# A seven-column sum moved into the unused columns of its neighbour tile, in a one-core attention and gated-convolution kernel

## The chip, the core and the metric

The kernel runs on one core of a Trainium2 chip. The metric is the device time of one execution in microseconds (us); the median of several runs counts, and lower is better. Engines are named as in the profile: PE multiplies matrices, PEld is its weight loading, DVE is the vector engine, ACT the scalar engine (activation functions and copies), POOL the general one, and SP issues all the DMAs.

## What is computed

For 8 batches of 12 heads, with 448 rows and a head width of 64, soft-capped attention is followed by a gated convolution and two projections of width 768. Cut to the core, the reference is:

```python
scores = scale * np.matmul(q, k.transpose(0, 1, 3, 2))
scores = cap * np.tanh(scores / cap)
attn = np.exp(scores - np.max(scores, axis=-1, keepdims=True))
attn = attn / (np.sum(attn, axis=-1, keepdims=True) + 1e-09)
x = np.matmul(attn, v)                 # heads side by side: (8, 448, 768)
gate = sigmoid(sum of conv_w[k] * x shifted by k rows, five taps)
out = (gate * (x @ w_val)) @ w_out
```

## The kernel before, in words

**Pairs and blocks.** Two heads make a pair of 128 partitions, so there are 48 pairs p, six to a batch. For each pair q and k are loaded by SP and turned by DVE (L455). The scores go through PE in four parts of 112 rows (L476), ACT takes tanh (L484) and exp (L488) of each part into a tile `pt`, and PE multiplies by v (L514). For pairs 0 to 12 the scores are plain float32 products of `qt` and `kt`; from pair 13 on, q and k are split into a high and a low half (`qh`, `ql`, `kh`, `kl`, the high halves by ACT at L461, the low ones by DVE at L390) and three faster products are added up. The sums of the exponentials over a row come from a product with ones (L530). For most pairs DVE first adds the four parts to one or two (`pa`, L498 and L495), so that PE has less to do there.

**The normalisation of a pair** is a short chain across DVE and POOL, and the change lies in it. `turn_sums` turns the 224 columns of sums into the tile `zt` (L536), which is 448 columns wide. `norm_recip` adds the guard 1e-9 to seven of these columns, one in 32 (L543, result `zc`), and takes the reciprocal of the seven twice over into `rc` (L544). `shift` lets POOL copy parts of `rc` between partitions (L551, L552), `spread` turns `rc` out over all 448 columns of `zt` (L557), and `norm_mul` multiplies the attention's output by it into `u` (L565). There are two tiles `u`, one for even pairs and one for odd ones.

**After the pair.** ACT rounds `u` to `xh` (L570), DVE takes the rest `xl` (L390), and DVE convolves five taps into a tile `gate` (L582 or L584, then four times L586). For each batch PE multiplies `xh` and `xl` by the first weights (L607 to L609, 448 columns each; the weights are the part that stays in the array, `xh` or `xl` the part that is streamed), DVE multiplies the result by the gate (L613), the gated values are split once more (`g_h` by ACT at L616, `g_l` by DVE at L390), and PE multiplies them by the second weights (L636 to L638, where 384 columns of `wo` are streamed). ACT copies the result to `osb` (L644) and SP stores it.

**What sets the order.** Three tables of numbers give every step of every pair, batch and weight block a due time; the steps are sorted by it and written to the engines' queues in that order. Each engine works through its queue strictly in order, and semaphores hold an instruction until its inputs are there. The change touches none of these tables.

**What sets the addresses.** A pool lays out its tiles in each partition in the order of the line that first asks for each name, with the number of buffers asked for, and rounds each tile up to a multiple of 32 bytes. In the pool `wk` the order is `qt`, `kt`, `pt` (6 buffers), `zt`, `rc`, `zc`, `gate` (7), `xh` (8), `xl` (8), `pa` (2) and `osb` (2). Behind this pool lie, first, the scratch tiles for the weights (`w_raw`, `w_late`, `w_t`), and later, in the same place, the halves `qh`, `kh`, `ql`, `kl`. Ahead of the pool lie the inputs' tiles, the weights `wv` and `wo`, the gated tiles `g_h` and `g_l`, and the tiles `u`.

The built program's addresses, taken modulo 64 bytes, fall into two classes. `zc` starts at byte 160672 of each partition and takes 32 bytes; the first `gate` follows at 160704, which is 2511 times 64. All tiles behind it are multiples of 64 bytes long where it matters (448 float32 are 28 times 64 bytes, 896 are 56 times), so `gate`, `xh`, `xl`, `pa`, `osb`, `qh`, `kh`, `ql`, `kl` and `w_raw` all start at a multiple of 64. Of the tiles ahead, `qt`, `kt`, `pt`, `zt`, `rc`, `zc`, `vn`, `ones`, `wv`, `wo`, `g_h`, `g_l` and the even pairs' `u` start 32 bytes past one, and the odd pairs' `u` starts at one.

The lines that the change and the prediction's steps touch:

Of the kernel before, what the change touches and what calls it, by code (L numbers as in the profile page):

```python
# [7 lines left out]
F32 = mybir.dt.float32  # L8
# [13 lines left out]
P = 128  # L22
# [326 lines left out]
def fast_path(tc, io, u2, q, k, v, w_val, conv_w, w_out, out, capt):  # L349
# [22 lines left out]
    HQ = S * BLK // D  # L372
    HC = HQ // BLK

    with ExitStack() as ctx:
        cpool = ctx.enter_context(tc.tile_pool(name="cpool", bufs=1))
        wk = ctx.enter_context(tc.tile_pool(name="wk", bufs=2))
# [160 lines left out]
        def norm_recip(p):  # L538
            st = state[p]
            rc = wk.tile([P, D // BLK, HC], F32, name="rc", bufs=1)  # L540
            zc = wk.tile([P, HC], F32, name="zc", bufs=1)
            col = st["zt"].rearrange("p (c e) -> p c e", e=BLK)[:, :HC, 0]
            nc.vector.tensor_scalar(zc, col, guard, None, ALU.add)  # L543
            nc.vector.reciprocal(rc, zc.unsqueeze(1).to_broadcast([P, D // BLK, HC]))  # L544
            st["rc"] = rc
# [109 lines left out]
        def at(when, f, *a):  # L655
# [7 lines left out]
            q_hi=lambda p: half_hi("q", p), k_hi=lambda p: half_hi("k", p),  # L663
            q_lo=lambda p: half_lo("q", p), k_lo=lambda p: half_lo("k", p),
            scores=scores, tanh=tanh, exp=exp, add=add, av=attnv, sums=sums, turn_sums=turn_sums, recip=norm_recip, shift=shift,
            spread=spread, mul=norm_mul, x_hi=x_hi, x_lo=x_lo, conv=conv,
        )
# [205 lines left out]
```

## Time and profile before

| what | value |
|---|---|
| median of 3 runs | 710.95 us (710.48 to 710.96) |
| the profiled execution's own time | 710.17 us |
| its span, first to last instruction | 708.3 us |
| PE busy | 689.1 us, 97% of the span |
| ACT busy | 576.5 us, 81% |
| DVE busy | 557.7 us, 79% |
| POOL busy | 76.6 us, 11% |

A row of the profile's groups names the line, the engine, the operation and its tiles as output<-inputs, then output and input shapes, the number of instructions, the union of their busy time in us and the mean time of one in ns, and behind the next bar the engine's idle time ahead of them with what ended it. For PE, durations overlap, since the next product enters the array before the last has left it: there the distance from start to start, in the timeline, is what an instruction costs. The chain of waits follows the execution back from its last instruction, at each step to what released it.

### The profile page before, as it was taken

Reading aid. Unit: us, or ns where it says so; the run is one execution under the profiler, and the core shown is the slowest. Engines: PE = TensorE matmul, PEld = TensorE weight load, DVE = VectorE, ACT = ScalarE, POOL = GpSimd, SP = SyncE. Lnnn points to the kernel's source line nnn. Section 1 sums busy time; section 2 is a strip of 40 time slices with the busy share of each in tenths; the row PEclk is TensorE's granted clock in tenths of the full one; section 3 lists DMA queues with packets and bytes.
Section 4 is the critical chain, followed back from the end, with each engine's and each line's share of the span. In section 5 each row is a group of like instructions: output and inputs, shape, how many; then the busy total and the mean of one; then the engine's idle time right before and its main releaser. Section 6 shows DMA issues by size and latency. Waiting matters only on the chain.

```text
span 708.3 us, 13291 instructions
## 1 busy us (share of the span) xinstructions
PE 689.1 (97%) x5024; PEld 481.2 (68%) x5024; DVE 557.7 (79%) x972; ACT 576.5 (81%) x738; POOL 76.6 (11%) x208
## 2 busy tenths in 40 slices
PE   5889999999999999999999999999999999999997
PEld 1233567567768776767768777587767867776997
DVE  1698999998798878987787887988889696887520
ACT  5999999898887798798895799879897689986211
POOL 0021101120001002100000010130001010120000
PEclk9999999999999999999999999999999999999999
DMA  7999998852415414134213352333323333101011
GB/s 138 175 217 217 225 219 187 226 112 55 76 27 122 81 32 82 35 86 88 64 30 72 87 107 47 53 72 67 64 51 53 95 65 64 38 25 45 12 35 58
DMA packets 241829, 63.88 MB, mean 90 GB/s; under 512 B 228448, under 2 KB 235616, under 8 KB 241760
## 3 DMA queue, kind: packets, MB, share of 16 engines
q1 hardware_dynamic: 241760, 62.98, 41.5%
q8 instruction: 41, 0.67, 0.4%
q14 instruction: 28, 0.23, 0.1%
HBM read 51.94 MB, written 11.01 MB: 89 GB/s over the span
## 4 chain that ended last, share of the span: by engine, by line
PE 85%; ACT 9%; SPq 2%; DVE 1%; DMA 1%; issue 1%; ACTq 0%
PE psa L514 17%; PE pss L476 16%; PE psf L607 9%; PE psf L636 8%; PE psf L608 8%; PE psf L609 8%; PE psf L638 8%; PE psf L637 8%; ACT pt L484 3%; ACT pt L488 3%; PE psz L530 2%; SPq L333 1%; ACT L488 1%; DMA qn<-in_q_dram 1%; SPq L307 1%
## 5 line engine op out<-in xcount | busy, mean ns | idle before, releaser
L484 ACT ACTIVATE pt<-pss,rc 112x896 f32<-112x896 f32 x192 | 187.9, 1003 | 39.8 <-PE pss L476 37.2
L488 ACT ACTIVATE pt<-pt,capt 112x896 f32<-112x896 f32 x192 | 194.5, 1042 | 1.2
L514 PE MATMUL psa<-pt,vn 112*32 112x448 f32 x1440 | 150.3, 542 | 0.0
L586 DVE SCALAR_TENSOR_TENSOR gate<-u,cw,gate 128x448 f32<-128x448 f32 x192 | 125.6, 663 | 1.0 <-ACT gate L582 0.2
L636 PE MATMUL psf<-wo,g_h 128*128 128x384 f32 x336 | 115.2, 343 | 0.0
L638 PE MATMUL psf<-wo,g_l 128*128 128x384 f32 x336 | 112.7, 335 | 0.2 <-DVE g_l L390 0.2
L637 PE MATMUL psf<-wo,g_h 128*128 128x384 f32 x336 | 112.5, 335 | 0.0
L607 PE MATMUL psf<-xh,wv 128*128 128x448 f32 x288 | 108.2, 376 | 0.1
L498 DVE TENSOR_TENSOR pa<-pt 112x896 f32<-112x896 f32 x84 | 90.9, 1086 | 19.9 <-ACT pt L488 19.6
L608 PE MATMUL psf<-xh,wv 128*128 128x448 f32 x288 | 105.8, 368 | 0.0
L609 PE MATMUL psf<-xl,wv 128*128 128x448 f32 x288 | 105.8, 367 | 0.0
L551 POOL COPY rc<-rc 32x7 f32<-32x7 f32 x96 | 33.2, 346 | 555.2 <-DVE rc L544 553.2
L514 PEld LDWEIGHTS psa<-pt,vn 112*32 112x32 f32 x1440 | 42.3, 109 | 71.6 <-issue 58.4
L636 PEld LDWEIGHTS psf<-wo,g_h 128*128 128x128 f32 x336 | 63.0, 188 | 10.1 <-issue 7.5
L644 ACT COPY osb<-psf 128x384 f32<-128x384 f32 x56 | 26.5, 477 | 45.6 <-PE psf L638 44.2
L638 PEld LDWEIGHTS psf<-wo,g_l 128*128 128x128 f32 x336 | 63.1, 188 | 0.5 <-DVE g_l L390 0.5
L607 PEld LDWEIGHTS psf<-xh,wv 128*128 128x128 f32 x288 | 54.0, 188 | 13.6 <-issue 5.8
L637 PEld LDWEIGHTS psf<-wo,g_h 128*128 128x128 f32 x336 | 63.1, 188 | 0.1
L476 PE MATMUL pss<-qt,kt 64*112 64x448 f32 x208 | 49.5, 587 | 12.6 <-DVE guard L399 7.9
L476 PE MATMUL pss<-qh,kh 64*112 64x448 f32 x280 | 58.0, 410 | 0.0
L609 PEld LDWEIGHTS psf<-xl,wv 128*128 128x128 f32 x288 | 54.0, 188 | 5.1
L608 PEld LDWEIGHTS psf<-xh,wv 128*128 128x128 f32 x288 | 54.1, 188 | 4.5
(76 smaller groups left out, 908.1 us busy)
## 6 DMA issues: line engine op xcount, KB each, us to landing
vn<-in_v_dram SPq DMA_DIRECT2D x96, 112.0 KB, 2.8
out_dram<-osb SPq DMA_DIRECT2D x56, 192.0 KB, 2.2
kn<-in_k_dram SPq DMA_DIRECT2D x188, 56.0 KB, 2.4
qn<-in_q_dram SPq DMA_DIRECT2D x188, 56.0 KB, 2.4
w_raw<-in_moe_w_val_dram SPq DMA_DIRECT2D x12, 384.0 KB, 3.9
w_late<-in_moe_w_val_dram SPq DMA_DIRECT2D x12, 384.0 KB, 4.2
w_raw<-in_moe_w_out_dram SPq DMA_DIRECT2D x12, 384.0 KB, 3.6
w_late<-in_moe_w_out_dram SPq DMA_DIRECT2D x12, 384.0 KB, 4.3
```

Source lines behind the costliest of these rows:

```text
L476: nc.tensor.matmul(ps[:CH, j, :S], st[x][r, c], st[y][r], start=(n == 0), stop=(n == len(parts) - 1))
L484: nc.scalar.activation(st["p", i], st.pop(("s", i)), AF.Tanh, scale=rc8[:CH])
L488: nc.scalar.activation(t, t, AF.Exp, scale=capt[:CH])
L498: nc.vector.tensor_tensor(st["a", i], st["p", 2 * i], st["p", 2 * i + 1], op=ALU.add)
L514: nc.tensor.matmul(st["o"][r, :S], vloads[p][:, j, i, d:d + BLK], t[:, j], start=(i == 0), stop=(i == NKT - 1))
L586: nc.vector.scalar_tensor_tensor(g, u[:, i:i + S], cw[:, hp, i:i + 1], g, ALU.mult, ALU.add)
L607: nc.tensor.matmul(o, w_h, xh, start=(c == 0), stop=False)
L608: nc.tensor.matmul(o, w_l, xh, start=False, stop=False)
L609: nc.tensor.matmul(o, w_h, xl, start=False, stop=(c == NCC - 1))
L636: nc.tensor.matmul(o, g_h[:, d, s], w_h, start=(d == 0), stop=False)
L637: nc.tensor.matmul(o, g_h[:, d, s], w_l, start=False, stop=False)
L638: nc.tensor.matmul(o, g_l[:, d, s], w_h, start=False, stop=(d == NCC - 1))
```

## The change

The guarded sums no longer have a tile of their own. They are written to columns 224 to 230 of `zt`, which hold nothing at that point: the turned sums fill columns 0 to 223, and `spread` writes all 448 columns later.

```diff
         def norm_recip(p):
             st = state[p]
             rc = wk.tile([P, D // BLK, HC], F32, name="rc", bufs=1)
-            zc = wk.tile([P, HC], F32, name="zc", bufs=1)
+            zc = st["zt"][:, HQ:HQ + HC]
             col = st["zt"].rearrange("p (c e) -> p c e", e=BLK)[:, :HC, 0]
             nc.vector.tensor_scalar(zc, col, guard, None, ALU.add)
             nc.vector.reciprocal(rc, zc.unsqueeze(1).to_broadcast([P, D // BLK, HC]))
```

`HQ` is 224 and `HC` is 7. The queue of DVE at the first pair, before (-) and after (+), with the engines that each instruction waits for in brackets:

```order
 L536 STREAM_TRANSPOSE zt<-psz 128x224 [waits PE_49]
-L543 TENSOR_SCALAR zc<-zt,guard 128x7 [waits DVE_49]
-L544 RECIPROCAL rc<-zc 128x14 [waits DVE_49]
+L543 TENSOR_SCALAR zt<-zt,guard 128x7 [waits DVE_49]
+L544 RECIPROCAL rc<-zt 128x14 [waits DVE_49]
 L557 STREAM_TRANSPOSE zt<-rc 128x448 [waits DVE_49,Pool_49]
```

Nothing moves here, and nowhere else: apart from the output of L543 and the input of L544, all 48 times, the two programs have the same instructions in the same order, with the same semaphores waited for up to the same counts.

What does move is addresses. With `zc` gone, every tile behind it starts 32 bytes earlier: the first `gate` at 160672 instead of 160704. So `gate`, `xh`, `xl`, `pa`, `osb`, `qh`, `kh`, `ql`, `kl` and the weights' scratch now start 32 bytes past a multiple of 64, as most tiles ahead of them do. The tiles ahead, and all tiles in the accumulation memory, stay where they were. The new place of the seven sums, byte 159712, is 32 past a multiple of 64, as the old one was.

## The prediction

> **What bounds the kernel now.** I read the page first, for which engine sets the end.
>
> ```profile
> span 708.3 us, 13291 instructions
> PE 689.1 (97%) x5024; PEld 481.2 (68%) x5024; DVE 557.7 (79%) x972; ACT 576.5 (81%) x738; POOL 76.6 (11%) x208
> PEclk9999999999999999999999999999999999999999
> PE 85%; ACT 9%; SPq 2%; DVE 1%; DMA 1%; issue 1%; ACTq 0%
> PE psa L514 17%; PE pss L476 16%; PE psf L607 9%; PE psf L636 8%; PE psf L608 8%; PE psf L609 8%; PE psf L638 8%; PE psf L637 8%; ACT pt L484 3%; ACT pt L488 3%; PE psz L530 2%; SPq L333 1%; ACT L488 1%; DMA qn<-in_q_dram 1%; SPq L307 1%
> ```
>
> PE is busy for 97% of the span, its granted clock is at the full digit in every slice, and 85% of the chain that ended last is PE. What PE needs for one product is therefore the time, nearly one for one, while DVE and ACT have a fifth of the span idle. The line that names DVE's part of the chain says 1%: L543 and L544, the two edited instructions, cannot matter much as work. The chain's shares of L607, L608 and L609 (9, 8 and 8%) are all products that stream tiles which the change moves (`xh`, `xl`); a part of L476 (`qh`, `ql`) and of L530 (`pa`) are the others.
>
> Since the order and every wait stay as they are, there are only two things to price: the two instructions that now read and write `zt`, and the address of everything behind `zc`.
>
> **The two instructions.** Their groups, two early instructions as a comparison, and the one wait for `zc` outside its own chain:
>
> ```profile
> L544 DVE RECIPROCAL rc<-zc 128x14 f32<-128x14 f32 x48 | 11.6, 242 | 1.6
> L543 DVE TENSOR_SCALAR zc<-zt,guard 128x7 f32<-128x7 f32 x48 | 10.7, 223 | 0.5
> L296 DVE TENSOR_SCALAR cw_t<-cw 128x30 int32<-128x30 int32 x1 | 0.2, 180 | 0.0
> L295 DVE TENSOR_SCALAR cw_m<-cw_m 128x30 int32<-128x30 int32 x1 | 0.2, 175 | 0.0
> PE pss L476 <- DVE zc L543: 1.8, 1, 1.8
> ```
>
> Writing into the tile that is read costs nothing there: a small operation of the same kind takes 175 ns in place and 180 ns into another tile. The difference over 48 instructions is 48 x 5 ns = 0.24 us in all, either way, on an engine that idles for a fifth of the span, and PE was held up behind L543 once in the whole run. I take 0.0 us, with 0.2 us as both ends. The cover is PE's own work: what hides this chain is that its result is due (L565, then `xh`) long before PE needs it at L607. Gone, it would cost its 48 x 5 ns and no more.
>
> **The addresses, on DVE and ACT.** The trace of before has both classes of address side by side in the same kinds of operation, so no guess is needed.
>
> ```profile
> L586 DVE SCALAR_TENSOR_TENSOR gate<-u,cw,gate 128x448 f32<-128x448 f32 x192 | 125.6, 663 | 1.0 <-ACT gate L582 0.2
> L498 DVE TENSOR_TENSOR pa<-pt 112x896 f32<-112x896 f32 x84 | 90.9, 1086 | 19.9 <-ACT pt L488 19.6
> L495 DVE TENSOR_TENSOR pa<-pa,pa 112x896 f32<-112x896 f32 x37 | 40.1, 1083 | 0.7
> L390 DVE TENSOR_TENSOR xl<-u,xh 128x448 fp32r<-128x448 f32 x48 | 29.2, 608 | 1.3 <-ACT xh L570 1.2
> L390 DVE TENSOR_TENSOR g_l<-gate,g_h 128x448 fp32r<-128x448 f32 x48 | 28.8, 612 | 2.7 <-ACT g_h L616 2.7
> L390 DVE TENSOR_TENSOR kl<-kt,kh 128x448 fp32r<-128x448 f32 x35 | 21.6, 621 | 5.2 <-ACT kh L461 5.1
> L390 DVE TENSOR_TENSOR ql<-qt,qh 128x448 fp32r<-128x448 f32 x35 | 21.2, 606 | 3.3 <-ACT qh L461 3.1
> L570 ACT CAST xh<-u 128x448 fp32r<-128x448 f32 x48 | 26.8, 560 | 10.1 <-DVE u L565 10.0
> L616 ACT CAST g_h<-gate 128x448 fp32r<-128x448 f32 x48 | 26.5, 559 | 18.8 <-DVE gate L613 18.8
> ```
>
> L498 reads tiles 32 bytes past a multiple of 64 and L495 reads tiles at one: 1086 against 1083 ns. `g_l` and `g_h` are written 32 past, `xl` and `xh` at a multiple: 612 against 608 ns on DVE, 559 against 560 ns on ACT. `kl` and `ql` have the same addresses modulo 64 and differ by 15 ns, so this is scatter. The largest group that moves, L586, has no such pair of rows; the spread of the four L390 rows, 606 to 621 ns or 1.2% either way of the middle, would be 1.5 us on its 125.6 us, spread over a DVE that idles 150 us. I take 0.0 us on both engines.
>
> **The addresses, in DMAs.** The stores read `osb`, and the weights' loads write `w_raw` and `w_late`, early in the run.
>
> ```profile
> out_dram<-osb SPq DMA_DIRECT2D x56, 192.0 KB, 2.2
> w_raw<-in_moe_w_val_dram SPq DMA_DIRECT2D x12, 384.0 KB, 3.9
> w_late<-in_moe_w_val_dram SPq DMA_DIRECT2D x12, 384.0 KB, 4.2
> L295 DVE TENSOR_SCALAR w_late<-w_late 128x768 int32<-128x768 int32 x12 | 6.7, 558 | 0.3 <-DMA w_late<-in_moe_w_out_dram 0.3
> ```
>
> `w_late` lands 2 bytes past a 32-byte place and `w_raw` at a multiple of 64, from the same source: 4.2 against 3.9 us, 0.3 us for 384 KB. That is the nearest row for what an odd place costs a transfer. A load's 0.3 us is hidden: DVE waited 0.3 us in all for the landing of `w_late`. A store has half the bytes, so up to 0.15 us, and only the last one is not hidden, since nothing follows it. So 0 to 0.15 us; I take 0, because 32 bytes are no odd place of that kind.
>
> **The addresses, on PE.** This is the term that decides. PE streams `pa` (L530), `qh` and `ql` (L476) and `xh` and `xl` (L607 to L609) from the moved places.
>
> ```profile
> L607 PE MATMUL psf<-xh,wv 128*128 128x448 f32 x288 | 108.2, 376 | 0.1
> L609 PE MATMUL psf<-xl,wv 128*128 128x448 f32 x288 | 105.8, 367 | 0.0
> L476 PE MATMUL pss<-qh,kh 64*112 64x448 f32 x280 | 58.0, 410 | 0.0
> L476 PE MATMUL pss<-ql,kh 64*112 64x448 f32 x280 | 51.4, 362 | 0.0
> L476 PE MATMUL pss<-qh,kl 64*112 64x448 f32 x280 | 51.4, 361 | 0.0
> L530 PE MATMUL psz<-pa,ones 112*32 112x224 f32 x376 | 26.2, 354 | 0.2 <-DVE pa L495 0.2
> L530 PE MATMUL psz<-pt,ones 112*32 112x224 f32 x96 | 6.5, 357 | 0.6 <-ACT pt L488 0.6
> L530 PE MATMUL psf<-pt,ones 112*32 112x224 f32 x96 | 6.3, 358 | 0.9 <-ACT pt L488 0.9
> ```
>
> L530 is one operation with both addresses: `pa` at a multiple of 64 takes 354 ns, `pt` 32 bytes past it takes 357 and 358 ns, which is 1.0% more. These durations are modelled and the two kinds stand at different places in the run, so 1.0% is the upper end of a loss, and I read it as none.
>
> The faster products (L607 on) have no such twin. The nearest are L636 to L638, which stream `wo` from 32 past a multiple of 64, but 384 columns of it. From start to start, in two stretches of the timeline in which PE did nothing else (the first and the last row of each):
>
> ```profile
> 659.65 0.37 PE L608 MATMUL psf<-xh,wv 128*128 128x448 f32 x1
> ...
> 661.50 0.37 PE L608 MATMUL psf<-xh,wv 128*128 128x448 f32 x1
> 479.81 0.33 PE L637 MATMUL psf<-wo,g_h 128*128 128x384 f32 x1
> ...
> 481.54 0.34 PE L638 MATMUL psf<-wo,g_l 128*128 128x384 f32 x1
> 302.02 0.36 PE L476 MATMUL pss<-ql,kh 64*112 64x448 f32 x2
> ...
> 302.84 0.36 PE L476 MATMUL pss<-qh,kl 64*112 64x448 f32 x2
> ```
>
> Nine steps of 448 columns take 1.85 us, 205.6 ns each; ten steps of 384 columns take 1.73 us, 173 ns each; four pairs of L476 take 0.82 us, 205 ns each. At the rate of `wo` 448 columns would take 173 x 448/384 = 201.8 ns. So streams from multiples of 64 are 3.8 ns, or 1.8%, dearer than by that measure, not cheaper. The rows bound the address's price on PE from both sides: a gain of at most 3.8 ns for each product, a loss of 1.0%. Neither end is shown to come from the address: length, and what stands in the array, differ too. I take 0.
>
> [...]
>
> **The sum.** 0.0 (two instructions) + 0.0 (DVE, ACT) + 0.0 (DMAs) + 0.0 (PE) = 0.0 us against the profiled execution's 710.17 us (its span of 708.3 and 1.87 around it). That execution is 0.78 us, 0.11%, below the median of the runs, so I forecast the median, 711.0 us. A measurement of this kernel can tell about 0.2%, 1.4 us, from no change: 709.5 to 712.4.
>
> **Rival B, faster: the faster products read more quickly from 32 past a multiple of 64.** If the 3.8 ns are the address's doing, all 3 x 288 = 864 products of L607 to L609 lose them, on the path whole: 864 x 3.8 ns = 3.3 us. L476's pairs, at 205 against 201.8 ns, 420 of them, would give 1.3 us more where PE isn't waiting. I price it without these: 710.95 - 3.3 = 707.7 us. For it: the dearer stream is the one at multiples of 64, and the other is even. Against it: L530 shows no gain from that side, only a loss.
>
> **Rival C, slower: a stream that starts off a multiple of 64 needs one access more.** Its place is the same products and L530, its price L530's 1.0%: 864 x 205.6 ns x 1.0% = 1.8 us, 420 pairs of L476 x 205 ns x 1.0% = 0.9 us, and 94 groups of four L530 x 3.5 ns = 0.3 us; together 3.0 us, 713.9 us. It decides from about 0.5% on, 1.4 us on the 264 us of these products. For it: the L530 rows. Against it: on DVE and ACT no row shows such an access, and `wo`, which starts off a multiple of 64, is the cheapest stream by the column. [...]
>
> **Rival D, the two instructions do cost.** L543 might be held until its read of `zt` has drained before it writes there, and L544 likewise: at the most twice their 223 and 242 ns, 48 x 465 ns = 22 us of DVE. But DVE has 150 us idle, and PE waited behind L543 once. A tenth on the path, 2.2 us, gives 713.2 us.
>
> **How the numbers follow.** No change has 0.71: all rows that have both addresses show none beyond scatter, and nothing is reordered. Rival B has 0.12 and rival C 0.14, each resting on rows about PE that can be read otherwise; rival D has 0.03. Hence faster 0.12, same 0.71, slower 0.17. No change alone holds 0.71, so the range goes on to rival C's whole price, 713.9, which takes in rival D, and on the other side to half of rival B's 3.3 us, 709.3.
>
> **What would show it.** L543 and L544 at 223 and 242 ns within 10, and no wait of PE on them. L586, L390, L498 and the casts within their scatter. If the steps of L607 to L609 are still 205 to 206 ns and `psz<-pa` is at 354 ns, rivals B and C both fall; 202 ns and a time near 707.7 would be B; 207 to 208 ns, `psz<-pa` at 357 to 358 and a time near 713.9 would be C. The forecast is wrong if the median lies outside 709.5 to 712.4 us, and its reason is wrong if DVE's or ACT's means move by over 2%.

## The result and the profile after

The kernel after takes 707.01 us (median of 6 runs, 706.16 to 707.25) against 710.76 us before (6 runs, 709.92 to 710.96, the three of the table above among them): the ratio is 0.9947, with a 95% interval of 0.9934 to 0.9960. That is 3.75 us, 0.53%, faster. The prediction of no change was wrong, and the time lies below 709.3 us, the low end of its range.

First the page of after, with the lines that answer to those of before:

```profile
span 705.2 us, 13291 instructions
PE 685.4 (97%) x5024; PEld 481.1 (68%) x5024; DVE 557.3 (79%) x972; ACT 576.1 (82%) x738; POOL 76.6 (11%) x208
PE 83%; ACT 11%; DVE 2%; DMA 1%; SPq 1%; issue 1%; POOL 0%; POOLq 0%; ACTq 0%
```

The span is 3.1 us shorter, and PE's busy time has fallen from 689.1 to 685.4 us, 3.7 us, with the same number of instructions; in both traces each engine starts its instructions in the same order (5024 on PE, 972 on DVE). DVE and ACT are where they were to 0.4 us. So the gain is to be looked for in what PE needs for its products.

Then the groups of after, for the products that stream moved tiles, the edited instructions, and DVE's largest group:

```profile
L607 PE MATMUL psf<-xh,wv 128*128 128x448 f32 x288 | 106.7, 371 | 0.2
L608 PE MATMUL psf<-xh,wv 128*128 128x448 f32 x288 | 104.5, 363 | 0.0
L609 PE MATMUL psf<-xl,wv 128*128 128x448 f32 x288 | 104.1, 361 | 0.0
L476 PE MATMUL pss<-ql,kh 64*112 64x448 f32 x280 | 51.7, 362 | 0.0
L530 PE MATMUL psz<-pa,ones 112*32 112x224 f32 x376 | 26.2, 354 | 0.2 <-DVE pa L495 0.2
L530 PE MATMUL psz<-pt,ones 112*32 112x224 f32 x96 | 6.5, 358 | 0.7 <-ACT pt L488 0.7
L543 DVE TENSOR_SCALAR zt<-zt,guard 128x7 f32<-128x7 f32 x48 | 10.7, 223 | 0.5
L544 DVE RECIPROCAL rc<-zt 128x14 f32<-128x14 f32 x48 | 11.6, 242 | 1.6
L586 DVE SCALAR_TENSOR_TENSOR gate<-u,cw,gate 128x448 f32<-128x448 f32 x192 | 125.5, 663 | 0.9
```

L607 to L609 are 5 to 6 ns shorter each (376, 368 and 367 ns before). The other rows shown are at their old means: 362 ns in L476, 354 (`pa`) and 358 (`pt`, 357 before) in L530, 223 and 242 for the two edited instructions, 663 in L586.

What such a product costs is read from start to start: in the trace of before 5008 of the 5024 products have not reached their modelled end when the next one starts. Near the end of the run stands an uninterrupted run of 99 of these products. Sixty steps of it in the timeline of before (first and last row):

```profile
662.11 0.37 PE L608 MATMUL psf<-xh,wv 128*128 128x448 f32 x1
...
674.43 0.37 PE L608 MATMUL psf<-xh,wv 128*128 128x448 f32 x1
```

and sixty steps of after:

```profile
662.05 0.36 PE L607 MATMUL psf<-xh,wv 128*128 128x448 f32 x1
...
674.05 0.36 PE L607 MATMUL psf<-xh,wv 128*128 128x448 f32 x1
```

12.32 us for sixty is 205.3 ns a step before, 12.00 us is 200.0 ns after. Of the 864 products 810 are followed by another of their kind in one go; 810 x 5.3 ns is 4.3 us. The span of the profiled execution shows 3.1 us of it (PE's busy time fell by 3.7, and its idle time, span less busy, grew from 19.2 to 19.8), and the median of the runs 3.75 us.

### The profile page after: what moved, and what is told of

Same layout as the page of the kernel before. It is cut to its first block, busy times and chain, and to the rows that moved or that the text cites. A ratio compares the mean times of both kernels' runs of the same rounds, so it can differ in the third digit from the quotient of the medians.

```text
span 705.2 us, 13291 instructions
## 1 busy us (share of the span) xinstructions
PE 685.4 (97%) x5024; PEld 481.1 (68%) x5024; DVE 557.3 (79%) x972; ACT 576.1 (82%) x738; POOL 76.6 (11%) x208
## 4 chain that ended last, share of the span: by engine, by line
PE 83%; ACT 11%; DVE 2%; DMA 1%; SPq 1%; issue 1%; POOL 0%; POOLq 0%; ACTq 0%
PE psa L514 16%; PE pss L476 16%; PE psf L636 8%; PE psf L607 8%; PE psf L638 8%; PE psf L637 8%; PE psf L608 8%; PE psf L609 7%; ACT pt L488 4%; ACT pt L484 4%; PE psz L530 2%; PE psf L514 1%; ACT L488 1%; DMA qn<-in_q_dram 1%; DVE pa L498 1%
## 5 line engine op out<-in xcount | busy, mean ns | idle before, releaser
L586 DVE SCALAR_TENSOR_TENSOR gate<-u,cw,gate 128x448 f32<-128x448 f32 x192 | 125.5, 663 | 0.9
L636 PE MATMUL psf<-wo,g_h 128*128 128x384 f32 x336 | 115.1, 343 | 0.0
L638 PE MATMUL psf<-wo,g_l 128*128 128x384 f32 x336 | 112.6, 335 | 0.4 <-DVE g_l L390 0.4
L607 PE MATMUL psf<-xh,wv 128*128 128x448 f32 x288 | 106.7, 371 | 0.2
L608 PE MATMUL psf<-xh,wv 128*128 128x448 f32 x288 | 104.5, 363 | 0.0
L609 PE MATMUL psf<-xl,wv 128*128 128x448 f32 x288 | 104.1, 361 | 0.0
L551 POOL COPY rc<-rc 32x7 f32<-32x7 f32 x96 | 34.7, 362 | 551.8 <-DVE rc L544 549.8
L636 PEld LDWEIGHTS psf<-wo,g_h 128*128 128x128 f32 x336 | 63.0, 188 | 10.0 <-issue 6.8
L638 PEld LDWEIGHTS psf<-wo,g_l 128*128 128x128 f32 x336 | 63.1, 188 | 0.7 <-DVE g_l L390 0.7
L607 PEld LDWEIGHTS psf<-xh,wv 128*128 128x128 f32 x288 | 54.0, 187 | 12.7 <-issue 6.1
L476 PE MATMUL pss<-qt,kt 64*112 64x448 f32 x208 | 49.3, 585 | 12.4 <-DVE guard L399 7.9
L476 PE MATMUL pss<-qh,kh 64*112 64x448 f32 x280 | 58.0, 409 | 0.0
L609 PEld LDWEIGHTS psf<-xl,wv 128*128 128x128 f32 x288 | 53.9, 187 | 3.7
```

Source lines behind the costliest of these rows:

```text
L476: nc.tensor.matmul(ps[:CH, j, :S], st[x][r, c], st[y][r], start=(n == 0), stop=(n == len(parts) - 1))
L586: nc.vector.scalar_tensor_tensor(g, u[:, i:i + S], cw[:, hp, i:i + 1], g, ALU.mult, ALU.add)
L607: nc.tensor.matmul(o, w_h, xh, start=(c == 0), stop=False)
L608: nc.tensor.matmul(o, w_l, xh, start=False, stop=False)
L609: nc.tensor.matmul(o, w_h, xl, start=False, stop=(c == NCC - 1))
L636: nc.tensor.matmul(o, g_h[:, d, s], w_h, start=(d == 0), stop=False)
```

## The experiments

After the result three theories stood. T1: a product's time hangs on where its own streamed tile starts, modulo 64 bytes (the mechanism of the prediction's rival B). T2: it hangs on the distance between the streamed tile and the weights. T3: another moved tile, or the two edited instructions, made the room. In all kernels "distance" is the start of the streamed part minus the start of the weights' part, modulo 256 bytes. The buffers of `xh` lie alternately at two places modulo 512 in every kernel but one, and both kinds show the same step (205.4 and 205.3 ns before), so no period of 512 shows. The unused tiles in the pool `wk` are made by a helper once each; the cuts show the lines in the order in which the tiles are laid out, and three dots stand for lines left out:

```python
def pad(name, n=32):
    if name not in pads:
        pads[name] = wk.tile([P, n // 4], F32, name=name, bufs=1)
```

### Only xh and xl moved

```diff
 # kernel before
+            pad("pad0")
             xh = wk.tile([P, S], F32R, name="xh", bufs=NXX)
...
+            pad("pad1")
             st["a", i] = wk.tile([CH, 2, S], F32, name=f"pa{i}", bufs=1)
```

> The kernel before, with zc where it was; a 32-byte tile that nobody uses ahead of xh and another behind xl, so that of the tiles in question only xh and xl start 32 past a multiple of 64 (all behind them moves by a full 64). T1 (a product's time hangs on where its own streamed tile starts): L607, L608 and L609 at 371, 363 and 361 ns as after the change, time near 707.0. T2 (it hangs on the streamed tile's place against the weights' place): the same, since both are then 32 past, as after the change. T3 (another moved tile, gate or the halves or pa, got out of the way): 376, 368 and 367 ns as before, time 710.8. That the edit of the two instructions gave the gain: 710.8.

Measured: 709.99 us, ratio 0.9986 (0.9976 to 0.9995); L607 to L609's counterparts at 374, 366 and 366 ns. Neither 707 nor 710.8. `xh` and `xl` do start 32 past a multiple of 64, as after the change, but their distance from the weights is 128 here, and not 64 as after the change: they moved up by 32 bytes, and the change moved them down. T1 with its modulus of 64 falls. Sixty steps of this kernel, 12.24 us, are 204.0 ns each:

```profile
662.09 0.36 PE L615 MATMUL psf<-xh,wv 128*128 128x448 f32 x1
...
674.33 0.36 PE L615 MATMUL psf<-xh,wv 128*128 128x448 f32 x1
```

### Everything moved but xh and xl

```diff
 # kernel after
+            pad("pad0")
             xh = wk.tile([P, S], F32R, name="xh", bufs=NXX)
...
+            pad("pad1")
             st["a", i] = wk.tile([CH, 2, S], F32, name=f"pa{i}", bufs=1)
```

> The kernel after the change, with a 32-byte unused tile ahead of xh and another behind xl: xh and xl are back at a multiple of 64, while gate, pa, osb and the halves stay 32 past one, and the two edited instructions stay edited. T1 and T2: L607 to L609 back at 376, 368 and 367 ns, time 710.5 to 710.9 (up to 0.6 us less through the halves in L476). T3, or a gain from the edited instructions: 371, 363 and 361 ns, time 707.0.

Measured: 710.49 us, ratio 0.9995 (0.9986 to 1.0004), and 376, 367 and 367 ns. With `xh` and `xl` back at their old place the gain is gone, although the edit is in place and `gate`, `pa`, `osb` and the halves start where they do after the change, modulo 64. T3 falls.

### Only xl moved

```diff
 # kernel before
+            pad("pad0")
             xl = wk.tile([P, S], F32R, name="xl", bufs=NXX)
...
+            pad("pad1")
             st["a", i] = wk.tile([CH, 2, S], F32, name=f"pa{i}", bufs=1)
```

> The kernel before, with an unused 32-byte tile between xh and xl and another behind xl, so that only xl starts 32 past a multiple of 64. T1: a third of the products gains, L609 at 361 ns, L607 and L608 at 376 and 368, time 709.4 (a third of the gain of 3.8 us). T2: the same. If a product's time hangs on the stream before or behind it instead, L607 or L608 gains and not L609.

Measured: 708.77 us, ratio 0.9966 (0.9952 to 0.9979). The gain of the means fell mostly on the product that streams `xh` just ahead of `xl`, at 363 ns (368 before); the one that streams `xl` is at 366 (367), the first at 374 (376). So a product's time is not a matter of its own streamed tile alone; its neighbour's place counts.

### Only the weights moved by 32, the rest by 64

```diff
 # kernel before
+        cpool.tile([P, 8], F32, name="pad0")
         wv = cpool.tile([P, NCC, 2, 2, NH], F32R, name="wv")
+        cpool.tile([P, 8], F32, name="pad1")
         wo = cpool.tile([P, NCC, 2, 2, NH], F32R, name="wo")
```

> The kernel before, with an unused 32-byte tile ahead of wv and another behind it: the weights of L607 to L609 start at a multiple of 64, as xh and xl do, and everything behind wv moves by a full 64. T1: nothing changes, 376, 368 and 367 ns, 710.8 us. T2: streamed tile and weights are in the same class again, so the gain comes as after the change, 371, 363 and 361 ns, 707.0 us. A place modulo 128 instead of 64 would also show here, since xh and xl move from 64 to 0 modulo 128.

Measured: 709.51 us, ratio 0.998 (0.9970 to 0.9989), 375, 366 and 366 ns. This was neither of the two values expected, but the distance is 128, as in the first experiment, with both tiles at other places; and the steps agree with it, down to their pattern (196, 203, 212, 200 and 209 ns in turn, the same within 1 ns in both). That spoke for T2 with a modulus of 256, or of 128.

### T2 put to the test from both sides: only the weights move

```diff
 # kernel before: wv 32 bytes up, all else by 256
+        cpool.tile([P, 8], F32, name="pad0")
         wv = cpool.tile([P, NCC, 2, 2, NH], F32R, name="wv")
+        cpool.tile([P, 56], F32, name="pad1")
         wo = cpool.tile([P, NCC, 2, 2, NH], F32R, name="wo")
```

> The kernel before, with xh and xl at their old places modulo 256 bytes and only wv moved, by 32 bytes (an unused tile of 32 bytes ahead of wv and one of 224 behind it, so that all others move by a full 256). The streamed tile then lies 64 bytes behind the weights modulo 256, as after the change, instead of 96. T2, by the distance between streamed tile and weights modulo 256: the whole gain, L607 to L609 at 371, 363 and 361 ns, time near 707.0. T1, by the streamed tile's own place: nothing, 376, 368 and 367 ns, 710.8.

The timeline of this kernel, sixty steps of the same run of products:

```profile
662.10 0.36 PE L609 MATMUL psf<-xh,wv 128*128 128x448 f32 x1
...
674.10 0.36 PE L609 MATMUL psf<-xh,wv 128*128 128x448 f32 x1
```

200.0 ns a step, and 707.5 us, ratio 0.9956 (0.9941 to 0.9970): the whole gain, with the seven sums in their own tile, and with `xh` and `xl` at their old places modulo 256. The counterpart takes the kernel after and moves `wv` back to the old distance (56 columns ahead of `wv`, 8 behind it):

> The kernel after the change, with wv moved 32 bytes down modulo 256 and everything else at its place after the change modulo 256: the distance is 96 again. T2: the gain is gone, L607 to L609 at 376, 368 and 367 ns, 710.8 us. T1: the gain stays, 371, 363 and 361 ns, 707.0 us.

```profile
662.14 0.37 PE L611 MATMUL psf<-xl,wv 128*128 128x448 f32 x1
...
674.46 0.37 PE L611 MATMUL psf<-xl,wv 128*128 128x448 f32 x1
```

205.3 ns a step, and 710.77 us, ratio 1.0003 (0.9994 to 1.0012): the gain is gone with the change in place. T2 stands, T1 is dead.

### The other products: wo moved by 96

```diff
 # kernel after
+        cpool.tile([P, 24], F32, name="pad0")
         wo = cpool.tile([P, NCC, 2, 2, NH], F32R, name="wo")
...
+        cpool.tile([P, 40], F32, name="pad1")
         gated = {i: cpool.tile([P, NCC, GW], F32R, name=f"g_{i}") for i in "hl"}
```

> The kernel after the change, with wo moved 96 bytes up modulo 256 and everything else in place modulo 256. In L636 to L638 wo is streamed against g_h and g_l; their distance is 0 in both kernels and 96 here. T2, if it holds for these products too: L636 to L638 become dearer by about 5 ns each, 1008 of them, so about 5 us slower than after the change, near 712. T1, or T2 for L607 to L609 alone: unchanged, 707.0 us.

The groups of this kernel:

```profile
L638 PE MATMUL psf<-wo,g_h 128*128 128x384 f32 x336 | 116.4, 346 | 0.0
L639 PE MATMUL psf<-wo,g_h 128*128 128x384 f32 x336 | 113.8, 339 | 0.0
L640 PE MATMUL psf<-wo,g_l 128*128 128x384 f32 x336 | 113.8, 339 | 0.4 <-DVE g_l L390 0.4
```

3 to 5 ns more each than after the change (343, 334 and 335 ns), and 709.11 us, ratio 0.9976 (0.9967 to 0.9986), 2.1 us above the kernel after. The rule holds for these products too, at some 3 ns and not the 5 that were expected.

### Eight distances in one kernel

```diff
 # kernel before
-            xh = wk.tile([P, S], F32R, name="xh", bufs=NXX)
+            xh = wk.tile([P, S + 8], F32R, name="xh", bufs=NXX)[:, :S]
...
-            xl = wk.tile([P, S], F32R, name="xl", bufs=NXX)
+            xl = wk.tile([P, S + 8], F32R, name="xl", bufs=NXX)[:, :S]
```

> The kernel before, with each of the 8 buffers of xh and of xl made 32 bytes longer, so that the buffers lie at 8 different distances from the weights: 96, 128, 160, 192, 224, 0, 32 and 64 bytes modulo 256. T2: the mean step of the products differs by buffer, about 205 ns at 96, 204 at 128, 200 at 64, and the other distances are new. T1 modulo 64: two classes that alternate from buffer to buffer.

One run: 709.52 us. The mean steps were 202.4, 203.5, 202.1, 204.5, 202.8, 204.4, 202.0 and 203.3 ns at distances 0, 32, 64 and so on to 224. It differs by buffer, but by less than expected, and the later kernels show that the mixture misled: at distance 160 it gave 204.4 ns, one distance at a time gives 200.0. That the place of the buffer before and behind counts as well is an estimate from the kernel where only `xl` moved (363 ns for the product ahead of the one that streams `xl`, 368 before).

### One distance at a time

Four kernels put `xh` and `xl` at one distance each, all other tiles at their places after the change modulo 256: an unused tile of 192, 128, 224 or 96 bytes ahead of `xh`, and the rest to 256 behind `xl`. The first of them:

```diff
 # kernel after
+            pad("pad0", 192)
             xh = wk.tile([P, S], F32R, name="xh", bufs=NXX)
...
+            pad("pad1", 64)
             st["a", i] = wk.tile([CH, 2, S], F32, name=f"pa{i}", bufs=1)
```

> The kernel after the change, with xh and xl moved so that they lie at distance 0 from the weights modulo 256 bytes, as wo does from g_h and g_l, and all other tiles at their places after the change modulo 256. If distances that are multiples of 64 are the cheap ones: steps of about 200 ns, L607 to L609 at about 371, 363 and 361 ns, 707.0 us. If distance 0 is the place of most collisions: dearer than before, over 376 ns, over 711 us. Mixed buffers gave 202.4 ns at 0 and 202.1 at 64, so I lean to the first.

> The same with xh and xl at distance 192. Mixed buffers gave 202.0 ns there, the lowest of all. If the cheap distances are multiples of 64: 707.0 us, within 0.5 us of the kernel after; a version that beats it would have to lie below 706.3.

> The same with xh and xl at distance 32, and so at a place that is a multiple of 64 in itself. If distances that are no multiples of 64 are the dear ones: steps of 204 to 205 ns, 375 to 376 ns for L607, 710 to 711 us. If 96 is a single bad distance: 707 us.

> The kernel after the change with xh and xl at distance 160. Mixed buffers gave 204.4 ns there, near the value at 96: about 204 to 205 ns a step in L607 to L609, 710 to 711 us. If the mixed buffers misled: anything down to 200 ns, 707.0 us.

All distances measured, with the step over sixty products of the same run near the end, the mean of L607 or its counterpart, and the time against the kernel before of the same chip:

| distance | kernels | step, ns | L607, ns | time, us | ratio to before |
|---|---|---|---|---|---|
| 0 | one at a time | 206.7 | 375 | 710.40 | 0.9991 (0.9982 to 1.0000) |
| 32 | one at a time | 206.7 | 374 | 709.92 | 0.9981 (0.9973 to 0.9990) |
| 64 | after; weights up | 200.0; 200.0 | 371; 371 | 707.01; 707.50 | 0.9947; 0.9956 |
| 96 | before; all but x; weights down | 205.3 each | 376 each | 710.76; 710.49; 710.77 | 1; 0.9995; 1.0003 |
| 128 | only x; only weights | 204.0 each | 374; 375 | 709.99; 709.51 | 0.9986; 0.9980 |
| 160 | one at a time | 200.0 | 371 | 706.69 | 0.9945 (0.9932 to 0.9957) |
| 192 | one at a time | 202.2 | 372 | 709.02 | 0.9967 (0.9954 to 0.9980) |

Sixty steps at distance 0, 12.40 us, and at distance 160, 12.00 us (first and last row of each):

```profile
662.09 0.37 PE L617 MATMUL psf<-xl,wv 128*128 128x448 f32 x1
...
674.49 0.37 PE L617 MATMUL psf<-xl,wv 128*128 128x448 f32 x1
662.13 0.36 PE L615 MATMUL psf<-xh,wv 128*128 128x448 f32 x1
...
674.13 0.36 PE L615 MATMUL psf<-xh,wv 128*128 128x448 f32 x1
```

Distance 224 was measured in the mixture alone. Kernels of the same distance agree, whichever tile was moved to reach it. "Multiples of 64 are cheap", to which I leaned, is wrong on both counts: 0 is dear and 160 is as cheap as 64. At 0 and 32 most uninterrupted runs of products settle at one of two paces, 202.6 or 206.6 ns at 0 and 200.0 or 206.6 ns at 32, and keep it until PE turns to something else; so the means over the kernel, 204.9 and 203.3 ns, lie below the step in the table. At 160 one of the 26 uninterrupted runs of nine or more products keeps 206.6 ns and the others 200.0, so the mean there is 200.4 ns, against 200.1 after the change.

### The scores' products

```diff
 # kernel after: kh and kl 32 bytes up, ql back in step
+            if name == "k":
+                kpad("pad2", 32)
             st[name, "h"] = scratch["qk"].tile([P, S], F32R, name=name + "h")
...
+            kpad(*(("pad3", 224) if name == "q" else ("pad4", 32)))
             st[name, "l"] = scratch["qk"].tile([P, S], F32R, name=name + "l")
```

> The kernel after the change, with kh and kl moved by 32 bytes against qh and ql; xh and xl stay at distance 64. In L476 qh and ql are streamed against kh and kl, at distances 0, 64, 128 and 192 by the part of the scores; here these become 32, 96, 160 and 224. If the rule holds for these products too, their 420 pairs become 3 to 5 ns dearer, 1.3 to 2.1 us at most on the time, 708.3 to 709.1. If not, or if PE waits there anyway: 707.0.

Measured: 706.63 us, ratio 0.9935 (0.9922 to 0.9948), so no slower than the kernel after. The pairs' mean step rose from 201.8 to 203.6 ns, less than expected. The other kernels, whose scores' products have the same distances as those of the kernel after, lie between 201.6 and 202.8 ns, so some of the 1.8 ns is scatter. Only 277 of the pairs' steps follow each other without a pause, and 277 x 1.8 ns is 0.5 us, too little to tell from the scatter of the runs (706.49 to 707.06 us).

### What makes distance 0 dear here and cheap in L636 to L638

```diff
-            o = psums[b, d][:, :S]
+            o = psums[b, d][:, :NH]
...
-                xh, xl = xs[b * NPAIR + c]
+                xh, xl = (x[:, :NH] for x in xs[b * NPAIR + c])
```

> The kernel with xh and xl at distance 0, but L607 to L609 stream only 384 of the 448 columns, and L613 multiplies only these (the last 64 columns of each tile miss the product with the first weights). At 448 columns distance 0 costs 205 ns a step. If the number of columns decides: about 173.5 ns, as in L636 to L638 at distance 0. If something else about these tiles does: 205 less 64 columns, about 178 ns.

> The same cut to 384 columns in the kernel before, where the distance is 96. If the number of columns decides: about 176.7 ns, as L636 to L638 took with wo moved to distance 96. If not: about 178.6 ns, the 205.3 ns of 448 columns less 64 columns.

This is the whole edit of the kernel at distance 96, but for L613, which multiplies only these columns. The kernel at distance 0 has the same edit on top of the kernel after with the unused tiles that gave distance 0. The groups with 384 columns at distance 0, then at 96:

```profile
L615 PE MATMUL psf<-xh,wv 128*128 128x384 f32 x288 | 98.9, 343 | 0.9 <-DVE gate L621 0.8
L616 PE MATMUL psf<-xh,wv 128*128 128x384 f32 x288 | 96.3, 334 | 0.0
L617 PE MATMUL psf<-xl,wv 128*128 128x384 f32 x288 | 96.5, 335 | 0.0
```

```profile
L607 PE MATMUL psf<-xh,wv 128*128 128x384 f32 x288 | 100.0, 347 | 0.9 <-DVE gate L613 0.7
L608 PE MATMUL psf<-xh,wv 128*128 128x384 f32 x288 | 97.5, 338 | 0.0
L609 PE MATMUL psf<-xl,wv 128*128 128x384 f32 x288 | 97.4, 338 | 0.0
```

These are, to 1 ns, the means of L636 to L638 at distance 0 (343, 335 and 335) and with `wo` moved to 96 (346, 339 and 339). The mean steps, 173.7 and 176.6 ns, agree as well. So, at these two distances, the number of columns and the distance together set the step; which tiles they are does not matter. (One run each: 698.75 and 699.09 us. They leave out the last 64 columns of these products, so their times say nothing of a gain.)

The last one asks whether 64 is better than 0 at 384 columns (in the kernel after, an unused tile of 64 bytes ahead of `wo` and 192 behind it):

> The kernel after the change with wo moved to distance 64 from g_h and g_l, all others in place modulo 256. If 64 is the good distance for every product, L636 to L638 stay at 173.5 ns or gain up to a few ns each of 1008, down to 704 us. If the good distance hangs on the number of columns: between 173.5 and 177 ns, 707 to 710 us.

Measured: 706.85 us, ratio 0.9943 (0.9931 to 0.9955), and a mean step of 173.3 ns, against 173.8 after the change. At 384 columns 0 and 64 are alike within what the runs can tell, and 96 is dearer; the other five distances were not tried there. No kernel tried is clearly faster than the one after: the three with the lowest medians, 706.63 to 706.85 us, have intervals that overlap its own.

## Why the prediction was wrong

**What bounds the kernel: right.** PE's time for one product went into the time nearly one for one: its busy time fell by 3.7 us, the span of the same two executions by 3.1, and the median of the runs by 3.75.

**The two instructions, DVE and ACT: right, at 0.0 us.** L543 and L544 stand at 223 and 242 ns as before, L586 at 663, and the kernel that keeps the edit and all other moves but those of `xh` and `xl` is the same as before (0.9995). The DMAs' term showed nothing either: the stores land after 2.1 us (2.2 before) and the loads of `w_raw` after 3.8 (3.9).

**The addresses, on PE: the step that failed.** "Neither end is shown to come from the address [...] I take 0." The rows had bounded the term, with a gain of at most 3.8 ns for each product; it was 5.3 ns, and the bound came out too small because it took the step to grow in proportion to the columns, where 64 columns more cost 200.0 - 173.3 = 26.7 ns and not 28.8. The choice of zero leaned on rows with both classes of address, and none of them could show the effect: all 5024 weight loads of the trace (LDWEIGHTS) are PEld's and none is DVE's or ACT's, so the rows of these two have no distance between a streamed tile and weights, and the L530 products are of another kind (plain float32, like the `qt`, `kt` products of L476 at 587 ns, not the faster products, at 361 to 410 ns there). L530's `psz<-pa` stayed at 354 ns when `pa` moved, and `psz<-pt`, now in the same class of address, is at 358; so its 1.0% was not the address, and rival C, which took its price from there, fell with it. The scores' products, which rivals B and C counted besides, could not have told either: their halves all moved by the same 32 bytes, and so kept their distances from each other. Their pairs take 202.3 ns on the mean of the kernel before, not the 205 ns of the short stretch that the prediction read.

**Rival B had the place and nearly the price, but not the cause.** It named the 864 products and 3.3 us, 707.7; measured were 3.75 us and 707.01. Its sign in the profile, the dear step of L607 to L609 beside the cheaper one by the column of L636 to L638, was the right one to look at; that the step is uneven tells nothing, since it is so after the change as well (197, 202 and 201 ns in turn), and at distance 0 it is even and dear (206, 207 and 207). That its price came out near is in part luck: a product gained 5.3 ns and not 3.8, but not all of the 4.3 us that this adds up to reached the time. Its cause, a start 32 past a multiple of 64, is refuted: with only `xh` and `xl` moved, to distance 128, the tiles start there too and the step is 204.0 ns, and at distance 160 they start at a multiple of 64 and it is 200.0. What I had sorted was each tile's own address; what counts is its distance from the weights.

**Rival D** needed L543 to be slower in place; it is not (223 ns before and after).

## What to carry to other kernels

In this kernel, where TensorE sets the time (PE is busy for 97% of the span) and loads new weights for each product (5024 LDWEIGHTS for 5024 products), an edit that dropped a tile of 32 bytes moved the time by 0.53% through the addresses behind it. Before such a difference is put down to the edit in a kernel like it, the step from start to start of the same products is to be compared, and the edit tried with an unused tile that restores the old places modulo 256 bytes; then the good distance can be had on purpose, as with the weights alone moved here (707.50 us). Which distance is good is to be measured for each number of columns: here it was 64 or 160 at 448 columns, and 0 or 64 of the three tried (0, 64 and 96) at 384.

## What the runs showed of the hardware

In these kernels the step of a product with 448 streamed columns is 200.0 to 206.7 ns by the distance of streamed tile and weights modulo 256 bytes, and that of one with 384 columns 173.3 to 176.6 ns, at a granted clock of 0.995 to 1.0 in every run. In the kernel in which only the weights moved, from distance 96 to 64, the step fell from 205.3 to 200.0 ns, so the place of the weights counts as well as that of the streamed tile. By what mechanism the distance sets the step, and why most uninterrupted runs of products at distances 0 and 32 keep one of two paces, no run shows.
